# Router columns on two hardware queues, one-hot tiles over eight places, and an earlier x: one edit to a fused attention and expert kernel

## The chip, the cores and the metric

The kernel runs on one core of a Trainium2 chip. The metric is the device time of one execution in microseconds. TensorE (PE) multiplies, VectorE (DVE), ScalarE (ACT) and GpSimd (POOL) work elementwise, and SyncE (SP) mostly issues transfers; ScalarE and GpSimd issue some too.

## The reference

The input x is 2048 rows of 448. One half is 16-head softmax attention (28 columns a head); the other routes every row to two of eight experts. A gate from x mixes them.

```python
g = sigmoid((x * gate_w).sum(-1))
qkv = x @ wqkv; p = softmax(q @ k.T * 28**-0.5); a = (p @ v) @ wo
logits = x @ w_gate                       # 8 columns, one an expert
topk_idx, topk_val = the two largest;  gates = softmax(topk_val)
b = sum over e of w_e * (silu(x @ w1[e]) @ w2[e])    # w1[e] 448x1792, w2[e] 1792x448
out = g * a + (1 - g) * b
```

## The kernel before

Matrix products are computed from high and low halves: ScalarE copies a tile into the type that TensorE multiplies (`_h`, `hi`, `xeh`), VectorE subtracts that from the original (`_l`, `lo`, `xel`), and three products are added up. TensorE's, VectorE's and ScalarE's instructions stand in the order in which the program writes them, in all of the part below. GpSimd's and SyncE's order in this part is made by a scheduler, and it can shift when the program changes.

**Start and projection of v.** Rows of x come in 16 tiles of 128 (`load_x`, on SyncE). Each is transposed on TensorE (`turn_x`) and split. One weight tile `wv_r`, four blocks of rows, holds the v columns of `wqkv` (448), the eight router columns `w_gate`, the gate column `gate_w` and a zero column. `rows4` loads a narrow matrix into the four blocks with three transfers: rows 0 to 383 as 128x3, and rows 384 to 447 twice, since the fourth block holds its 64 rows two times; a last argument picks some of the three. Blocks 0 and 1 of the v columns come over ScalarE's queue, 2 and 3 over SyncE's, router and gate columns over GpSimd's. While this loads, `busy` issues transposes of a constant (7, 3 and 5) between the first two x tiles. ScalarE then splits the four blocks (`wv_h`, L336), VectorE makes their low halves (`wv_low`, L320), and eleven matmuls (L354) make v and the logits of one x tile.

**q and k, with the routing between.** `qk_tile(mt)` makes 128 columns of q and k for all rows in four chunks of 512 rows, eleven matmuls a chunk (L557), into one of four `pq` banks. ScalarE copies the bank (`hi`, L566), and VectorE's difference (`lo`, L569) is put off to the next chunk (`late`, `pop`). In the first 16 chunks (mt 3, 4, 0, 1) there are two places a chunk, behind its second and its fifth matmul, where `pop(1)` and `route(5)` run. `route` takes up to five steps of the generator `routing` and ends early where that yields "pause". `routing` picks two experts for each row, gives each row a slot, and then finds for every slot its row: for two choices and two halves of the tiles it compares a counting row with slot numbers into two one-hot tiles, `ob` (place in a block of 128, L480) and `ot` (block, L484), multiplies `ot` by the tile number on GpSimd (L487) and by the row's place on ScalarE (L489), and after some empty places four batches of eight matmuls (L500) add these up into the index lists.

**The first expert's x.** After these chunks five `gather` transfers fetch the first expert's rows (576 of them), and three more q/k tiles follow (mt 5, 2, 6). In the last one `first_x(c)` runs behind each of its four chunks and turns gathered tiles (`x_tile`, L217): four transposes on TensorE, a copy on ScalarE (L219), and the low halves on VectorE (L159, L160) at the next opportunity.

**Experts and attention.** For each expert there are two halves of seven hidden blocks (L797) and then the second product (L841), with row maxima for the attention (L101, L116) threaded between. w2's tiles come in a ring of nine (L663). Attention follows (L963, L975), then the output product (L921).

Of the kernel before, what the change touches and what calls it, by code (L numbers as in the profile page):

```python
# [24 lines left out]
S, D, H, DH, E, FF = 2048, 448, 16, 28, 8, 1792  # L25
# [19 lines left out]
def bc(ap, shape):  # L45
    return ap.to_broadcast(shape)
# [3 lines left out]
def tile_gated_mha_moe(ctx: ExitStack, tc: tile.TileContext, x, wqkv, wo, wgate, w1, w2, gw, out):  # L50
    nc = tc.nc
# [141 lines left out]
    def rows4(dst, src, eng, parts=slice(0, 3)):  # L193
        for to, rows in ((dst[:, 0:3], src[0:384].rearrange("(b p) n -> p b n", p=128)),
                         (dst[0:64, 3], src[384:448]), (dst[64:128, 3], src[384:448]))[parts]:
            eng.dma_start(to, rows)
# [7 lines left out]
    def first_w():  # L204
        return pe.tile([128, 4, 512], F32, name="wv_r")
# [6 lines left out]
    def x_tile(xg, k, new_pt, xeh, xel):  # L212
        n = CT[k]
        flush_x()
        pt = new_pt()
        for b in range(4):
            nc.tensor.transpose(pt[:, b, :n], xg[:n, b * 128:(b + 1) * 128], ident[:n, :n])  # L217
        h, l = xeh[:, :, k * 128:k * 128 + n], xel[:, :, k * 128:k * 128 + n]
        nc.scalar.activation(h, pt[:, :, :n], AF.Copy)  # L219
        late_x.append(lambda: split_xl(pt, h, l, n))  # L220

    with ExitStack() as pa:
# [8 lines left out]
        def load_x(t):  # L231
            xt = wk.tile([128, 512], F32, name="xt", bufs=NXT)
            nc.sync.dma_start(xt[:, 0:D], x[t * 128:(t + 1) * 128])
            xts.append(xt)

        wv_r = first_w()[:, :, 0:NV]
# [2 lines left out]
        nc.gpsimd.memset(warm, 0.0)  # L239
        load_x(0)  # L240
        load_x(1)
        for b in range(2):
            nc.scalar.dma_start(wv_r[:, b, 0:D], wqkv[b * 128:(b + 1) * 128, 2 * D:3 * D])
        nc.scalar.activation(warm[:, 1:2], warm[:, 0:1], AF.Copy)
        nc.sync.dma_start(wv_r[:, 2, 0:D], wqkv[256:384, 2 * D:3 * D])
        for b in range(2):
# [2 lines left out]
        nc.gpsimd.iota(jp, pattern=[[1, 128]], base=0, channel_multiplier=-1,  # L249
                       allow_small_or_imprecise_dtypes=True)  # L250
        nc.vector.tensor_scalar(ident, jp, 0.0, None, op0=ALU.is_equal)
        rows4(wv_r[:, :, D:D + E], wgate, nc.gpsimd)
        rows4(wv_r[:, :, D + E:D + E + 1], gw.unsqueeze(1), nc.gpsimd, slice(1, 3))
        nc.gpsimd.memset(wv_r[:, :, NV - 1], 0.0)
        for t in range(2, NXT - 1):
            load_x(t)
# [84 lines left out]
        for t in range(NT):  # L341
# [13 lines left out]
            if 4 <= t < 12:  # L355
                b, c = divmod(t - 4, 2)
# [28 lines left out]
        def routing():  # L385
# [90 lines left out]
            for c in range(2):  # L476
                for h in range(2):
                    hs_ = slice(8 * h, 8 * h + 8)
                    ob = wk.tile([128, 8, 128], BF, name="xt", bufs=NXT)
                    nc.vector.tensor_tensor(ob, bc(iob.unsqueeze(1), [128, 8, 128]),  # L480
                                            bc(bb[:, c, hs_].unsqueeze(2), [128, 8, 128]), op=ALU.is_equal)
                    yield
                    ot = sb.tile([128, 8, NTL], BF, name="ot", bufs=2)
                    nc.vector.tensor_tensor(ot, bc(iob[:, 0:NTL].unsqueeze(1), [128, 8, NTL]),  # L484
                                            bc(tb[:, c, hs_].unsqueeze(2), [128, 8, NTL]), op=ALU.is_equal)
                    mv = wk.tile([128, 8, 2, NTL], BF, name="xt", bufs=NXT)
                    nc.gpsimd.tensor_tensor(mv[:, :, 0], ot, bc(iot[:, hs_].unsqueeze(2), [128, 8, NTL]),  # L487
                                            op=ALU.mult)
                    nc.scalar.mul(mv[:, :, 1], ot, iop)  # L489
                    pairs.append((ob, mv))  # L490
                    yield "pause"
            yield "pause"
            yield "pause"
            yield "pause"
            yield "pause"
# [40 lines left out]
            yield "end"  # L536

        rt = routing()

        def route(n):  # L540
# [41 lines left out]
        xe = []  # L582

        def first_x(c):
            for k in ((0, 1), (2,), (3,), (4,))[c]:
                x_tile(xgs[k], k, lambda: ps.tile([128, 4, 128], F32, name="pt"), *xe)

        maxes(1)
# [461 lines left out]
```

## Time and profile before

| What | Value |
|---|---|
| median of 3 runs | 1495.57 us (1494.75 to 1496.4) |
| the profiled execution | 1493.23 us |
| its span, first to last instruction | 1491.4 us |
| TensorE busy | 99% of the span |
| VectorE, ScalarE, GpSimd busy | 54%, 59%, 41% |
| mean granted TensorE clock | 0.996 |

A row of the timeline has the start in us, the length, the engine, the line, the operation, what is written and read, the shape, how often it stands in a row, and in brackets the idle time of the engine before it and what ended that. A q behind an engine's name marks the issue of a transfer. A row of the waits has the engine and line that waited, what it waited for, and total us, times and longest. The chunk numbers in the prediction count the q/k chunks from 0.

### The profile page before, as it was taken

How to read it: one execution, taken by the hardware profiler on the slowest of the kernel's cores; microseconds unless marked ns; L12 is line 12 of the kernel's file. 1: busy time of each engine (PE TensorE's matmuls, PEld its weight loads, DVE VectorE, ACT ScalarE, POOL GpSimd, SP SyncE). 2: the span in 40 equal slices, each digit the busy share in tenths (PEclk: the TensorE clock that was granted, in tenths of full speed). 3: DMA queues.
4: the chain of work that ended last, by engine and by line, in shares of the span. 5: the costliest groups of instructions: out<-in, count | busy, mean ns of one | idle time of the engine just before them, and what ended most of it. 6: DMA issues, size and time to landing. Idle time of an engine off the chain costs nothing. (4 is left out here: it accounts for less than half of the span.)

```text
span 1491.4 us, 28369 instructions
## 1 busy us (share of the span) xinstructions
PE 1473.6 (99%) x11380; PEld 984.5 (66%) x11380; DVE 806.7 (54%) x672; ACT 882.3 (59%) x1539; POOL 613.8 (41%) x667
## 2 busy tenths in 40 slices
PE   8999999999999999999999999899999999999998
PEld 7878788788888887887888888533333333333348
DVE  4644777777768777767777777311122111123245
ACT  5324354344334433543443344399999999999981
POOL 2123575476457546754764565111113111214330
PEclk9999999999999999999999999999999999999999
DMA  9777631343233143313422410300221121143212
GB/s 322 259 250 233 177 96 55 106 123 96 76 120 114 42 124 120 96 54 107 126 84 73 120 60 1 92 21 21 68 66 52 54 66 34 29 112 107 71 37 103
DMA packets 107958, 147.97 MB, mean 99 GB/s; under 512 B 17356, under 2 KB 83308, under 8 KB 107824
## 3 DMA queue, kind: packets, MB, share of 16 engines
q1 hardware_dynamic: 98192, 124.90, 27.0%
q0 software_dynamic: 9344, 20.78, 4.8%
q8 instruction: 90, 1.47, 0.4%
q10 hardware_dynamic: 288, 0.46, 0.1%
q14 instruction: 44, 0.36, 0.1%
HBM read 108.56 MB, written 37.51 MB: 98 GB/s over the span
## 5 line engine op out<-in xcount | busy, mean ns | idle before, releaser
L116 DVE TENSOR_REDUCE mp<-pm 128x6 f32<-128x3072 f32 x171 | 573.1, 3351 | 141.7 <-PE pm L101 141.2
L966 ACT ACTIVATE P<-ps 128x1536 f32<-128x1536 f32 x256 | 370.7, 1448 | 0.0
L975 PE MATMUL po<-P,V 128*32 128x512 f32 x2048 | 273.7, 606 | 0.0
L797 PE MATMUL acc<-xeh,w1l 128*128 128x288 f32 x880 | 258.2, 300 | 0.0
L797 PE MATMUL acc<-xeh,w1h 128*128 128x288 f32 x880 | 257.3, 299 | 0.0
L714 POOL TENSOR_TENSOR w2l<-w2r,w2h 128x448 fp32r<-128x448 f32 x112 | 128.9, 1151 | 235.8 <-ACT w2h L708 204.9
L963 PEld LDWEIGHTS ps<-Q,Kh 29*128 29x128 f32 (+1 forms) x2048 | 79.4, 184 | 216.2 <-ACT P L965 215.7
L799 ACT ACTIVATE hh<-acc 128x288 fp32r<-128x288 f32 x224 | 92.1, 411 | 178.4 <-PE acc L797 178.4
L797 PE MATMUL acc<-xel,w1h 128*128 128x288 f32 x660 | 197.1, 299 | 0.0
L963 PE MATMUL ps<-Q,Kh 29*128 29x512 f32 (+1 forms) x2048 | 192.6, 446 | 1.6 <-ACT P L965 1.5
L930 POOL DMA_DIRECT2D sum_d<-osb x64 | 31.9, 509 | 353.6 <-DVE osb L979 353.6
L797 PEld LDWEIGHTS acc<-xeh,w1l 128*128 128x128 f32 x880 | 166.1, 189 | 14.4 <-issue 14.2
L841 PE MATMUL acc<-w2h,hh 128*128 128x448 f32 x448 | 171.4, 383 | 2.3 <-DMA Kh<-neg_d 2.3
L797 PEld LDWEIGHTS acc<-xeh,w1h 128*128 128x128 f32 x880 | 165.9, 189 | 11.2 <-issue 11.0
L841 PE MATMUL acc<-w2l,hh 128*128 128x448 f32 x448 | 169.3, 378 | 0.0
L841 PE MATMUL acc<-w2h,hl 128*128 128x448 f32 x448 | 165.9, 370 | 0.0
L979 DVE COPY osb<-po 128x512 f32<-128x512 f32 x16 | 11.1, 691 | 283.2 <-PE po L975 283.2
L965 ACT ACTIVATE P<-ps 128x512 f32<-128x512 f32 x256 | 153.0, 598 | 7.0 <-PE ps L963 6.2
L679 POOL TENSOR_TENSOR w1l<-w1r,w1h 128x512 fp32r<-128x512 f32 (+1 forms) x88 | 137.8, 1566 | 19.2 <-ACT w1h L673 6.9
L723 POOL TENSOR_TENSOR hl<-hf,hh 128x512 fp32r<-128x512 f32 x112 | 143.2, 1286 | 0.0
L797 PEld LDWEIGHTS acc<-xel,w1h 128*128 128x128 f32 x660 | 124.7, 189 | 7.9 <-issue 7.7
L101 PE MATMUL pm<-khg,qg 28*128 28x512 f32 x1024 | 124.9, 460 | 1.1 <-DVE mp L116 1.0
(179 smaller groups left out, 1855.3 us busy)
## 6 DMA issues: line engine op xcount, KB each, us to landing
w2r<-in_B_w_dram SPq DMA_DIRECT2D x112, 224.0 KB
w1r<-in_B_w_dram SPq DMA_DIRECT2D x56, 384.0 KB
w1r<-in_B_w_dram SPq DMA_DIRECT2D x112, 64.0 KB
qkh_d<-hi SPq DMA_DIRECT2D x28, 256.0 KB
qkl_d<-lo SPq DMA_DIRECT2D x28, 256.0 KB
ys_d<-yo SPq DMA_DIRECT2D x32, 224.0 KB
ys_d<-zf SPq DMA_DIRECT2D x24, 224.0 KB
v_d<-v_s SPq DMA_DIRECT2D x16, 256.0 KB
```

Of the source, the lines that this page charges most:

```text
L101: nc.tensor.matmul(pm[:, n], qgs[g, qt // 4][rw, (qt % 4) * 128:(qt % 4 + 1) * 128], kh[g, kc][rw], start=True, stop=True)
L116: nc.vector.tensor_reduce(mps[b // 48][:, o:o + len(step)], pm[:, 0:len(step)], axis=AX.X, op=ALU.max)
L679: nc.gpsimd.tensor_tensor(l[:, :, half], r[:, :, half], h[:, :, half].bitcast(F32), op=ALU.subtract)
L714: nc.gpsimd.tensor_tensor(w2l, w2r, w2h.bitcast(F32), op=ALU.subtract)
L723: nc.gpsimd.tensor_tensor(hl, hf32, hh[:, 0:512].bitcast(F32), op=ALU.subtract)
L797: nc.tensor.matmul(pu[:, 0:HC], a, b[:, cs], start=i == 0, stop=i == len(mms) - 1)
L799: nc.scalar.activation(hh[:, cs], pu[:, 0:HC], AF.Silu)
L841: nc.tensor.matmul(py[:n, 0:w], a[:, cs], b, start=i == 0, stop=i == 3 * NH - 1)
L963: nc.tensor.matmul(p3[:, j - 1] if j else p1, k[rw, ks], qs[u][rw, c], start=i == 0, stop=i == 2)
L965: nc.scalar.activation(P[:, 0], p1, AF.Exp, scale=SCALE)
L966: nc.scalar.activation(P[:, 1:4], p3, AF.Exp, scale=SCALE)
L975: nc.tensor.matmul(po[32 * j:32 * j + 32], v[:, kt % 8, 32 * j:32 * j + 32], P[:, j], start=kt == 0, stop=kt == NT - 1)
```

## The change

Three edits. First, of the router's three transfers into `wv_r`, the one for blocks 0 to 2 moves from GpSimd's queue to ScalarE's, between its two weight blocks, and the two for block 3 move to SyncE's, behind block 3 of the weights and ahead of x tile 2. The gate column's last two stay on GpSimd's queue. Second, the one-hot routine pauses after `ob` as well as after `ot`, so that the four pairs are spread over eight places instead of four, and one of the five empty places behind them is gone: the four batches of index matmuls come three places later. Third, `first_x` turns gathered tiles 2 and 3 behind the second chunk and tile 4 behind the third, and none behind the last.

```diff
-        for b in range(2):
-            nc.scalar.dma_start(wv_r[:, b, 0:D], wqkv[b * 128:(b + 1) * 128, 2 * D:3 * D])
+        nc.scalar.dma_start(wv_r[:, 0, 0:D], wqkv[0:128, 2 * D:3 * D])
+        rows4(wv_r[:, :, D:D + E], wgate, nc.scalar, slice(0, 1))
+        nc.scalar.dma_start(wv_r[:, 1, 0:D], wqkv[128:256, 2 * D:3 * D])
...
-        rows4(wv_r[:, :, D:D + E], wgate, nc.gpsimd)
         rows4(wv_r[:, :, D + E:D + E + 1], gw.unsqueeze(1), nc.gpsimd, slice(1, 3))
+        rows4(wv_r[:, :, D:D + E], wgate, nc.sync, slice(1, 3))
...
                     nc.vector.tensor_tensor(ob, bc(iob.unsqueeze(1), [128, 8, 128]),
                                             bc(bb[:, c, hs_].unsqueeze(2), [128, 8, 128]), op=ALU.is_equal)
-                    yield
+                    yield "pause"
...
                     pairs.append((ob, mv))
                     yield "pause"
-            yield "pause"
             yield "pause"
...
         def first_x(c):
-            for k in ((0, 1), (2,), (3,), (4,))[c]:
+            for k in ((0, 1), (2, 3), (4,), ())[c]:
                 x_tile(xgs[k], k, lambda: ps.tile([128, 4, 128], F32, name="pt"), *xe)
```

## The prediction

> **What bounds the kernel now.** I read the page first, then the waits of TensorE, then the timeline of the first 140 us, which is all that the change touches.
>
> ```profile
> PE 1473.6 (99%) x11380; PEld 984.5 (66%) x11380; DVE 806.7 (54%) x672; ACT 882.3 (59%) x1539; POOL 613.8 (41%) x667
> ```
>
> TensorE is busy for 1473.6 of 1491.4 us, and the change neither adds nor removes a matmul. So it can pay only through the 18 us in which TensorE stands, and through the clock. The waits of TensorE say where it stands (total us, times, longest):
>
> ```profile
> PE acc L841 <- DMA Kh<-neg_d: 2.3, 1, 2.3
> PE pq L557 <- DVE lo L569: 2.3, 1, 2.3
> ...
> PE acc L797 <- DVE xeh L160: 1.4, 1, 1.4
> ...
> PE acc L797 <- ACT ht L805: 0.3, 1, 0.3
> PE pq L354 <- DVE xel L320: 0.2, 1, 0.2
> ```
>
> The second row is the one-hot stage, the third the hand-over to the first expert, the last the start: one wait for each part of the change. The first row is the seam before attention, which is not touched. Everything from the first expert on keeps its instructions, so what TensorE gains before it should arrive at the end.
>
> **Part 1, the start.** The timeline, by start and length:
>
> ```profile
> 2.54 1.90 POOL L196 DMA_DIRECT2D wv_r<-in_B_w_gate_dram  x3
> 4.40 1.07 POOL L196 DMA_DIRECT2D wv_r<-in_gate_w_dram  x2
> 5.97 1.06 PE L316 MATMUL pt<-ident,xt 128*128 128x128 f32 x4
> 6.83 1.27 PE L325 MATMUL pq<-ident 128*128 128x128 f32 x5
> 6.93 0.29 DVE L160 TENSOR_TENSOR xh<-pt,xh 64x128 fp32r<-64x128 f32 x1
> 7.64 1.54 ACT L336 ACTIVATE xeh<-wv_r 128x458 fp32r<-128x458 f32 x3 [1.32 <-DMA wv_r<-in_B_w_gate_dram]
> 8.26 1.80 DVE L320 TENSOR_TENSOR xel<-wv_r,xeh 128x458 fp32r<-128x458 f32 x3 [1.03 <-ACT xeh L336]
> 9.02 0.47 PE L354 MATMUL pq<-xel,xh 128*128 128x458 f32 x1
> 10.17 0.37 PE L354 MATMUL pq<-xeh,xh 128*128 128x458 f32 x1
> 10.22 0.59 ACT L336 ACTIVATE xeh<-wv_r 128x458 fp32r<-128x458 f32 x1 [1.05 <-DMA wv_r<-in_gate_w_dram]
> 10.38 0.37 PE L354 MATMUL pq<-xel,xh 128*128 128x458 f32 x1
> 11.85 0.60 PE L316 MATMUL pt<-ident,xt 128*128 128x128 f32 x4
> ```
>
> The router's columns are issued by GpSimd at 2.54 and land at 7.64, where ScalarE has waited 1.32 us for them; the last gate column, issued from 4.40, lands at 10.22, after another 1.05. Without the first wait ScalarE splits blocks 0 to 2 in 6.32 to 7.86. VectorE is free at 6.93+0.29 = 7.22 and starts its three at 0.60 each there instead of at 8.26. But TensorE's filler transposes (L325) run until 6.83+1.27 = 8.10 and do not move. So the first projection matmul moves only to 8.10; the second, at 9.02 now, follows it. TensorE is still at about half speed there: four transposes take 1.06 us at 5.97 and 0.60 at 11.85. I take two matmuls at 0.42 and nine at 0.21 (10.17 to 10.38): 8.10+0.84+1.89 = 10.83, where the next transposes start now at 11.85. Gain 1.0 us.
>
> This needs the fourth block split before the tenth matmul, some 10.4. GpSimd no longer issues the three router transfers, so the two gate transfers move from 4.40 to 2.54; landing 1.9 earlier is 8.3, ScalarE is done at 8.9, VectorE by 9.7. It holds with 0.7 to spare. If only the filler's end counts, the gain is 0.2; that is the lower end, 1.1 the upper.
>
> What pays: ScalarE's queue gets one transfer of 384 rows of 32 bytes between its two weight blocks. No row of this size is on a hardware queue here. The queue itself gives the bound:
>
> ```profile
> q10 hardware_dynamic: 288, 0.46, 6.7%
> ```
>
> That is ScalarE's queue in the first 20 us: 6.7% of 16 engines is 21.4 us for 288 packets, 74 ns for one, nearly all of 1,792 bytes. 384 short rows at no more than 74 ns on 16 engines are 1.8 us; I take 0.5, since they are far shorter, from nothing to 1.8 for the range. The two weight blocks need 21.4/16 = 1.3 us of the engines, twice that beside SyncE's queue, so block 1 is in by about 5 (an estimate) and then by 5.5 to 7; it is wanted at 6.8. SyncE issues two small transfers more ahead of x tiles 2 to 7, some 0.9 us at 0.46 each (4.14 us for nine w2 loads, below); tile 2 is first wanted by the transposes at 11.85. I cost both at nothing, since the cover is the filler on TensorE and the two tiles that are in; with that cover gone up to 0.9 of the 1.0 is given back.
>
> The scheduler also moves two of the first expert's w1 loads from ahead of the v stores to behind them; wanted only from the expert's third hidden block on, they cost nothing, and what they free early I do not count.
>
> The Trainium skill speaks against this edit (DMA: Bandwidth & Descriptors, Specifications): transfers below 512 bytes run under line rate, by a read-modify-write. No run here shows 32-byte rows on these queues.
>
> **Part 2, one-hot tiles over eight places.** Timeline of VectorE, ScalarE and TensorE, then the windows (us, busy of five engines, granted clock, DMA share, GB/s):
>
> ```profile
> 67.92 0.68 DVE L484 TENSOR_TENSOR ot<-iob,tb 128x512 bf16<-128x512 bf16 x1
> 72.47 0.69 DVE L569 TENSOR_TENSOR lo<-pq,hi 128x512 fp32r<-128x512 f32 x1 [1.28 <-ACT hi L566]
> 74.81 1.21 DVE L480 TENSOR_TENSOR xt<-iob,bb 128x1024 bf16<-128x1024 bf16 x1
> 75.94 1.53 DVE L484 TENSOR_TENSOR ot<-iob,tb 128x512 bf16<-128x512 bf16 x1
> 78.75 1.89 DVE L569 TENSOR_TENSOR lo<-pq,hi 128x512 fp32r<-128x512 f32 x3 [1.27 <-ACT hi L566]
> 103.60 0.69 DVE L569 TENSOR_TENSOR lo<-pq,hi 128x512 fp32r<-128x512 f32 x1 [1.80 <-ACT hi L566]
> ```
> ```profile
> 77.51 0.72 ACT L489 ACTIVATE xt<-ot,iop 128x512 bf16<-128x512 bf16 x1 [1.86 <-DVE ot L484]
> 78.14 1.55 ACT L566 ACTIVATE hi<-pq 128x512 fp32r<-128x512 f32 x3
> ```
> ```profile
> 75.13 0.62 PE L500 MATMUL pt<-xt 128*128 128x128 bf16 x8
> 75.56 0.47 PE L557 MATMUL pq<-xh,wqk_l 128*128 128x512 f32 x1
> ...
> 79.49 0.50 PE L557 MATMUL pq<-xh,wqk_h 128*128 128x512 f32 x1 [2.30 <-DVE lo L569]
> ```
> ```profile
> 80.00:82.00 2.00, 2.00 (x13) 1.33 (x13) 1.02 (x3) 0.60 (x1) 0.00 (x0) 0.63 0.98 371
> 82.00:84.00 2.00, 2.00 (x12) 1.81 (x12) 0.30 (x1) 0.00 (x0) 0.00 (x0) 0.51 1.00 381
> ```
>
> A chunk of q/k takes 1.80+0.69 = 2.49 us (steady state). There are four pq banks, so chunk n+4 needs `lo` of chunk n. Now two one-hot pairs stand between two `lo`: on ScalarE the copy `hi` of chunk 5 stands behind the multiply at 77.51, which waits for the `ot` of 75.94. `lo` of chunk 5 is done at 79.4, and chunk 9 stands 2.30 us for it. Behind this the clock is at 0.63 and 0.51: 2 x 0.37 + 2 x 0.49 = 1.7 us lost.
>
> After: `ob`, then `ot`, at places of their own, and one `lo` for each pair. The ring of one chunk is ob 1.21, ot 0.68, multiply 0.72, hi 0.52, lo 0.69: 3.8 us against 2.49, so VectorE still falls behind by 1.3 a chunk, for four chunks. On the old clock `lo` of chunk 4 ends at 67.92+0.68+0.72+0.52+0.69 = 70.5, then 74.3, 78.1 and 82.0 for chunk 7. Chunk 9 would start at 79.49-2.30-0.43 = 76.8 (the batch at 75.13, 0.43 to the next row, comes three places later). Chunk 8 starts at 74.3, chunk 10 at 79.2; chunk 11, with two batches in chunk 10, at 82.6. Chunk 8 has 3.8 us to spare, then 2.5, 1.1 and 0.6. No wait is left, so neither is the slow clock: 2.3+1.7 = 4.0 us. The moved index matmuls put the gathers behind chunk 12 instead of 11, which without the 4 us is no later than now; they are needed only behind chunk 24.
>
> The Trainium skill (TensorE: Matmul & The Clock Gate, Part 1: The HAM clock gate) has the clock fall after an idle window of about 3.4 us, of windows that run freely. By that a 2.3 us wait alone costs no clock and the sum would be 4.1; the trace, with the slow clock right behind the wait, says 5.8.
>
> **Part 3, x a chunk sooner.**
>
> ```profile
> 132.13 0.46 PE L217 MATMUL pt<-ident,xg 64*128 64x64 f32 x4
> 133.58 0.23 DVE L160 TENSOR_TENSOR xeh<-pt,xeh 64x64 fp32r<-64x64 f32 x1
> 133.84 0.69 DVE L569 TENSOR_TENSOR lo<-pq,hi 128x512 fp32r<-128x512 f32 x1
> 133.96 0.37 PE L797 MATMUL acc<-xeh,wv_r 128*128 128x288 f32 x1 [1.36 <-DVE xeh L160]
> 135.88 4.14 SPq L663 DMA_DIRECT2D w2r<-in_B_w_dram  x9
> 138.37 0.58 ACT L708 ACTIVATE w2h<-w2r 128x448 fp32r<-128x448 f32 x1 [1.99 <-DMA w2r<-in_B_w_dram]
> 139.66 0.40 PE L797 MATMUL acc<-xeh,wv_r 128*128 128x288 f32 x1 [0.26 <-ACT ht L805]
> ```
>
> The fifth x tile is turned behind the last q/k chunk, and the expert waits 1.36 us for its split. Turned a chunk sooner, that split hides under 2.49 us of matmuls, and the expert starts 1.36 earlier. Next late is w2: its first load is issued at 135.88, 1.35 after the last `lo`, lands 2.49 later, and ScalarE's split of it stands ahead of the output that frees the accumulator. `lo` no longer stands behind the x split (one half of it is 0.23; I take 0.6 for both halves and their wait). In the built order SyncE's read of the spill count, which stands in the 1.35 us, moves behind w2's loads, and one key load more comes ahead of them. Together w2 comes some 0.8 sooner. TensorE arrives 1.36 sooner: the wait of 0.26 grows to 0.8. Net 0.8 us, from 0.5 (w2 no sooner than its `lo`) to 1.4.
>
> **Sum.** 1.0+4.0+0.8 = 5.8 us. The profiled execution took 1493.23 (span 1491.4), so it would be 1487.4. It lies 2.3 below the median of the timed runs, 1495.57, and I forecast for that: 1489.8.
>
> **The rivals.** One: the wait goes, but the clock had not followed it, or does not in the timed runs because its windows fall otherwise. Then 4.1: 1491.5. For it: how a 2.3 us wait falls on such windows is chance, and the profile is one execution. Against it: the only other wait of 2.3 us, at the seam, is followed by slow clock too.
>
> ```profile
> 954.00:958.00 4.00, 3.55 (x19) 2.07 (x17) 0.62 (x1) 0.42 (x1) 2.34 (x5) 0.57 0.12 38
> ```
>
> Chance 0.18. Two: the ring does not close. The `ot` at 75.94 took 1.53 where another took 0.68; with 0.85 more in each of four rings `lo` of chunk 7 ends at 85.4 and chunk 11 stands 2.8, with the slow clock behind: gain 1.0+0.8-0.5 = 1.3, 1494.3. It decides once a ring is over 0.15 us longer than mine. Against it: the long `ot` is the second of two pairs back to back, with GpSimd's product of the first beside it, and pairs now lie apart. Chance 0.07. Three: only the one-hot part arrives, start and hand-over being made up by transfers: 1491.6, chance 0.05. Four, slower: the short rows clog ScalarE's queue and block 1 comes late. Now it is split by 8.2 (7.64 and one of three); later than that, each us is one of TensorE's. To end 3 us slower against 4.8 from the other parts it must land near 16, eleven us late over 24 rows on each engine: 0.46 us a row against the 74 ns above. Then 1498.6, chance 0.04.
>
> **How the numbers follow.** The forecast keeps 0.66: 1489.8. About 0.2% (3.0 us) is what a measurement can tell, so faster is below 1492.6. Forecast and rivals one and three make 0.89, less 0.05 for a seam whose slow stretches fall differently: 0.84. Same 0.10 (rival two and part of that), slower 0.06. The low end is 1.1+4.0+1.4 with 1.7 for a slow stretch lost at the seam, 8.2: 1487.3, rounded to 1487.0. The high end, 1494.0, reaches nearly to rival two.
>
> **What would show it.** Right: the next transposes near 10.8 instead of 11.85; no row for `lo` among TensorE's waits and a clock of 1.00 from 60 to 100 us; no wait for xeh at the first expert, and one for ht near 0.8. Wrong: a wait for `lo` at chunk 10 or 11, ScalarE waiting for a weight block, or slow clock behind none of these.

## The result and the profile after

The changed kernel takes 1489.51 us (median of seven runs), the kernel before beside it 1494.94: a gain of 5.4 us where 5.8 was forecast. The ratio is 0.9967, 95% interval 0.9956 to 0.9977, which is 3.4 to 6.6 us. One run of the seven was disturbed and is left out of the ratio; the other six lie between 1487.65 and 1492.17, with a median of 1489.35. The profiled execution took 1489.51, its span is 1487.7, 3.7 less than before. The total agrees with the forecast; the parts do not all, and the third did not come.

TensorE's busy time, then its waits (total us, times, longest), in the changed kernel. The wait of L841 is the seam before attention, which was there before:

```profile
PE 1472.2 (99%) x11380; PEld 982.8 (66%) x11380; DVE 805.7 (54%) x672; ACT 883.1 (59%) x1539; POOL 611.7 (41%) x664
...
PE acc L841 <- DMA m_d<-mr: 2.3, 1, 2.3
...
PE acc L797 <- ACT ht L805: 1.4, 1, 1.4
...
PE pq L355 <- DVE xel L321: 0.2, 1, 0.2
```

The rows for `lo` (2.3) and for xeh (1.4) are gone. The wait for ht is 1.4 where it was 0.3 and where I forecast 0.8: a new wait has taken the place of the third edit's.

The start, timeline of the changed kernel (its lines from L243 to L490 are one higher than before):

```profile
1.16 0.45 ACTq L196 DMA_DIRECT2D wv_r<-in_B_w_gate_dram  x1
2.54 1.11 POOL L196 DMA_DIRECT2D wv_r<-in_gate_w_dram  x2
6.78 0.71 PE L326 MATMUL pq<-ident 128*128 128x128 f32 x5
6.98 1.54 ACT L337 ACTIVATE xeh<-wv_r 128x458 fp32r<-128x458 f32 x3 [0.50 <-DMA wv_r<-in_gate_w_dram]
7.62 0.47 PE L355 MATMUL pq<-xeh,xh 128*128 128x458 f32 x1
8.73 0.59 ACT L337 ACTIVATE xeh<-wv_r 128x458 fp32r<-128x458 f32 x1 [0.21 <-DMA wv_r<-in_B_w_gate_dram]
10.49 0.60 PE L317 MATMUL pt<-ident,xt 128*128 128x128 f32 x4
```

The transposes stand at 10.49 instead of 11.85 (forecast 10.83). What ends ScalarE's wait at 6.98 is now the gate column: its first transfer, rows 0 to 383, is issued by GpSimd at 1.28 in both kernels. The filler ends at 6.78+0.71 = 7.49 and not at 8.10: in this execution the clock was full from 6.41, before from 8.85.

The one-hot stage, VectorE and TensorE, and one row of the windows:

```profile
66.55 0.68 DVE L485 TENSOR_TENSOR ot<-iob,tb 128x512 bf16<-128x512 bf16 x1
68.51 0.69 DVE L569 TENSOR_TENSOR lo<-pq,hi 128x512 fp32r<-128x512 f32 x1 [1.28 <-ACT hi L566]
72.22 0.69 DVE L569 TENSOR_TENSOR lo<-pq,hi 128x512 fp32r<-128x512 f32 x1 [1.28 <-ACT hi L566]
75.92 0.69 DVE L569 TENSOR_TENSOR lo<-pq,hi 128x512 fp32r<-128x512 f32 x1 [1.27 <-ACT hi L566]
79.62 1.89 DVE L569 TENSOR_TENSOR lo<-pq,hi 128x512 fp32r<-128x512 f32 x3 [1.28 <-ACT hi L566]
```
```profile
75.10 0.39 PE L557 MATMUL pq<-xh,wqk_h 128*128 128x512 f32 x1
```
```profile
80.00:84.00 4.00, 4.00 (x30) 3.10 (x29) 2.20 (x4) 1.16 (x3) 0.00 (x0) 1.00 0.87 331
```

A ring takes 3.70 us from one `lo` to the next (forecast 3.8), no `ot` takes 1.53 any more, chunk 9 starts at 75.10 without a wait, TensorE is busy for all of 80 to 84 and the clock is 1.00.

The hand-over to the first expert:

```profile
127.07 0.29 PE L797 MATMUL acc<-xeh,wv_r 128*128 128x288 f32 x1
127.95 0.69 DVE L569 TENSOR_TENSOR lo<-pq,hi 128x512 fp32r<-128x512 f32 x1 [1.55 <-ACT hi L566]
129.04 0.87 SPq L85 DMA_DIRECT2D khg<-qkh_d  x2
130.01 4.15 SPq L663 DMA_DIRECT2D w2r<-in_B_w_dram  x9
132.57 0.58 ACT L708 ACTIVATE w2h<-w2r 128x448 fp32r<-128x448 f32 x1 [3.15 <-DMA w2r<-in_B_w_dram]
133.59 0.23 ACT L805 ACTIVATE ht<-acc 128x64 f32<-128x64 f32 x1
133.86 0.40 PE L797 MATMUL acc<-xeh,wv_r 128*128 128x288 f32 x1 [1.40 <-ACT ht L805]
```

The expert starts right behind the last chunk. Then ScalarE stands 3.15 us for w2, with the copies that free the accumulator queued behind that split, and TensorE stands 1.40.

What was won up to here did not all reach the end. Three marks of TensorE (start of the first q/k matmul, from there to the first of chunk 24, from there to the start of the last matmul of L797), in us, for all profiles of this study:

```
kernel                                first q/k  to chunk 24  to last L797
before                                    53.09        67.13        808.58
changed                                   51.72        62.94        808.29
changed, once more                        52.18        62.94        810.25
before + queues alone                     51.59        67.16        809.25
before + one-hot alone                    53.02        62.96        808.49
before + x alone                          53.15        65.58        810.37
before + filler in the wait               53.08        65.58        807.70
before + index matmuls later              52.84        66.11        808.42
changed, x as before                      52.58        62.96        808.36
changed, w2 split later                   51.93        62.93        808.30
changed, gate column moved                52.46        62.93        810.10
changed, both of these                    51.78        62.93        811.12
changed, w2 split later, w1 first         54.48        62.96        806.67
the last, x as before                     51.56        62.96        807.79
```

In the changed kernel's profile that is 1.37+4.19+0.29 = 5.85 us up to the last of L797, and 3.7 at the end. Part of the 2.1 between is the clock at the seam. First a row of the kernel before, then the changed kernel in windows cut where the clock changes:

```profile
961.00:965.00 4.00, 4.00 (x32) 1.17 (x28) 0.00 (x0) 2.48 (x4) 1.89 (x2) 0.57 1.00 204
```
```profile
945.08:948.49 3.41, 1.23 (x6) 1.16 (x7) 0.00 (x0) 1.28 (x1) 0.00 (x0) 1.00 0.15 38
948.49:951.90 3.41, 3.06 (x17) 1.63 (x15) 0.62 (x1) 0.32 (x1) 2.24 (x5) 0.50 0.12 38
951.90:955.32 3.42, 2.41 (x20) 1.51 (x24) 0.00 (x0) 3.03 (x4) 3.12 (x7) 0.50 0.89 222
955.32:958.73 3.41, 3.41 (x28) 1.00 (x24) 0.00 (x0) 2.47 (x3) 1.58 (x2) 0.50 1.00 211
```

Three windows of 3.41 us are at half clock, where the profile before has two (954.35 to 957.76 and 961.17 to 964.59). A whole window of matmuls at half clock costs 1.7 us, but TensorE stands for 1.4 us of these three. Compared at the same matmul, the changed kernel loses 0.7 us at the seam, 0.9 in attention, where its profile has two waits for `P` (at 1346.42 and 1373.47) that the one before has not, and the last 0.6 in the output product, whose matmuls follow each other a little more slowly. Why the last two losses came is open. How the seam falls matters in every comparison: two profiles of this study have no slow window there (x alone, and the filler below), and they come out of it 2.8 and 2.9 us sooner than the one before.

### The profile page after: what moved, and what is told of

Read it like the earlier page. It is cut to its first block, busy times and chain, and to the rows that moved or that the text cites. A ratio compares the mean times of both kernels' runs of the same rounds, so it can differ in the third digit from the quotient of the medians.

```text
span 1487.7 us, 28372 instructions
## 1 busy us (share of the span) xinstructions
PE 1472.2 (99%) x11380; PEld 982.8 (66%) x11380; DVE 805.7 (54%) x672; ACT 883.1 (59%) x1539; POOL 611.7 (41%) x664
## 3 DMA queue, kind: packets, MB, share of 16 engines
q8 instruction: 90, 1.47, 0.4%
## 5 line engine op out<-in xcount | busy, mean ns | idle before, releaser
L797 PE MATMUL acc<-xeh,w1l 128*128 128x288 f32 x880 | 258.0, 300 | 0.0
L797 PE MATMUL acc<-xeh,w1h 128*128 128x288 f32 x880 | 257.2, 299 | 0.0
L797 PE MATMUL acc<-xel,w1h 128*128 128x288 f32 x660 | 197.0, 298 | 0.0
L797 PEld LDWEIGHTS acc<-xeh,w1l 128*128 128x128 f32 x880 | 166.0, 189 | 14.4 <-issue 14.2
L841 PE MATMUL acc<-w2h,hh 128*128 128x448 f32 x448 | 171.3, 382 | 2.3 <-DMA m_d<-mr 2.3
L797 PEld LDWEIGHTS acc<-xeh,w1h 128*128 128x128 f32 x880 | 165.8, 188 | 11.2 <-issue 11.0
L841 PE MATMUL acc<-w2l,hh 128*128 128x448 f32 x448 | 169.0, 377 | 0.0
L841 PE MATMUL acc<-w2h,hl 128*128 128x448 f32 x448 | 165.7, 370 | 0.0
L797 PEld LDWEIGHTS acc<-xel,w1h 128*128 128x128 f32 x660 | 124.6, 189 | 7.9 <-issue 7.7
```

The costliest lines, as they stand in the source:

```text
L797: nc.tensor.matmul(pu[:, 0:HC], a, b[:, cs], start=i == 0, stop=i == len(mms) - 1)
L841: nc.tensor.matmul(py[:n, 0:w], a[:, cs], b, start=i == 0, stop=i == 3 * NH - 1)
```

## The experiments

Each ratio is to the kernel before that ran beside it. It is not the quotient of the two medians given, and can differ from that by about 0.001.

**The one-hot edit alone** (kernel before).

```diff
-                    yield
+                    yield "pause"
...
-            yield "pause"
```

> The kernel before with the one-hot edit alone. Theory (the wait for lo at chunk 9 goes and the slow clock behind it too): no row for lo among TensorE's waits, granted clock 1.00 from 60 to 100 us, chunk 24 starts about 4.0 us sooner than before's 120.22, time 4.0 us below before (ratio 0.9973). Rival (the slow clock at 80 us is not the wait's doing): the wait goes, a slow stretch of 3.4 us stays somewhere between 70 and 90 us, 2.3 us below before (0.9985). The start stays at 11.85 us for the second set of transposes, the expert still waits about 1.4 us for xeh.

Measured: 1489.2 against 1492.57, ratio 0.9966 (0.9952 to 0.9979). No wait for `lo`, 62.96 us from the first q/k matmul to chunk 24 instead of 67.13, which is 4.17. This part carries most of the gain. Whether the clock belongs to it, the next runs tell.

**The queues alone** (kernel before with the first block of the diff).

> The kernel before with the edit of the queues alone. Theory (the first projection matmul follows the gate column and the filler, not the router's columns): ScalarE's first split of a weight block starts near 7.0 us instead of 7.64, the second set of transposes starts at 10.5 to 10.8 us instead of 11.85, chunk 9 still waits about 2.3 us for lo, and 1.0 to 1.4 us below before (ratio 0.9991 to 0.9993). Rival (the start is set by where the first clock window falls, not by the transfers): the transposes' place differs from 11.85 by as much as the clock's change to full speed differs, and the time is that of before within 0.5 us.

Measured: 1491.71 against 1492.57, ratio 0.9990 (0.9981 to 0.9999). The first split starts at 6.88, the transposes at 10.38, and the first q/k matmul 1.5 sooner. The rival is out: in four profiles without this edit the clock was full by 6.74 and the transposes still stood at 11.60 to 11.91. The landing scatters, though: in five profiles with the edit the first split started at 6.83 to 7.15, in two at 7.86 and 8.19, as late as before.

**x alone** (kernel before).

```diff
-            for k in ((0, 1), (2,), (3,), (4,))[c]:
+            for k in ((0, 1), (2, 3), (4,), ())[c]:
```

> The kernel before with the first expert's x turned a chunk sooner, alone. Theory (w2's landing behind ScalarE's in-order split takes the gain back): the first expert matmul starts 1.3 us sooner relative to the last q/k chunk, but its fourth group of matmuls waits about 1.4 us for ht instead of 0.26, so net 0.2 to 0.3 us. Rival (as I forecast it): w2 lands 0.8 us sooner, the wait for ht is 0.8, net 0.8 us; at most 1.4 if no later wait grows.

Measured: 1493.44 against 1492.57, ratio 1.0004 (0.9995 to 1.0014): no gain. The wait for ht was 2.08, and the clock was at half behind it. The same profile shows a second thing. Here are windows of 3.41 us, cut where the clock can change, of the kernel before, of the queues alone and of x alone; all three wait 2.3 us for `lo`:

```profile
77.12:80.53 3.41, 1.11 (x12) 0.77 (x11) 2.14 (x4) 2.18 (x4) 1.04 (x1) 1.00 0.26 99
80.53:83.95 3.42, 3.42 (x17) 2.61 (x15) 0.79 (x2) 0.60 (x1) 0.00 (x0) 0.50 1.01 382
```
```profile
75.28:78.70 3.42, 1.11 (x6) 0.42 (x5) 2.15 (x4) 2.18 (x4) 1.20 (x2) 1.00 0.22 81
78.70:82.11 3.41, 3.41 (x21) 2.73 (x19) 1.14 (x2) 0.60 (x1) 0.00 (x0) 0.50 0.99 375
```
```profile
74.48:77.90 3.42, 2.78 (x18) 1.84 (x16) 3.08 (x3) 1.03 (x2) 2.11 (x2) 1.00 0.44 124
77.90:81.31 3.41, 1.73 (x13) 1.20 (x13) 1.89 (x3) 2.19 (x5) 0.83 (x1) 1.00 0.46 176
81.31:84.72 3.41, 3.41 (x28) 2.75 (x28) 1.31 (x2) 0.88 (x2) 0.00 (x0) 1.00 1.01 381
...
135.92:139.34 3.42, 1.34 (x10) 1.11 (x9) 2.90 (x1) 2.02 (x7) 1.34 (x2) 1.00 0.91 273
139.34:142.75 3.41, 3.41 (x16) 3.25 (x14) 0.00 (x0) 2.09 (x7) 2.52 (x3) 0.50 0.88 314
```

The second column is TensorE's busy time, the third from the right the clock. In the first two kernels the wait lies in one window (1.11 busy, 2.30 idle), and the next window is at half clock. In the third the window's edge cuts it into 0.64 and 1.68, and the clock stays full. The wait for ht, 2.08 idle in one window, is followed by half clock. So the 1.7 us are the wait's doing, but only where the wait falls into one window.

**A filler in the wait** (kernel before).

```diff
+                if (mt, c) == (0, 1):
+                    fill = ps.tile([128, 4, 128], F32, name="pt")
+                    for b in range(16):
+                        nc.tensor.transpose(fill[:, b % 4], ident, ident)
```

> The kernel before with 16 transposes of the identity (0.15 us each at full clock, 2.4 us) put into TensorE's order ahead of chunk 9, into a buffer nobody reads: they fill the wait for lo and leave its length. Theory (the slow clock at 80.5 to 83.9 us follows from the idle TensorE): chunk 9 starts at about 79.5 as before, the granted clock stays at 1.00 from 60 to 100 us, and chunk 12 starts 1.7 us sooner than before's 90.30; 1.7 us below before (ratio 0.9989). Rival (the slow stretch has another cause, for example where the clock's windows fall): the slow stretch stays, time as before within 0.3 us.

```profile
77.02 1.91 PE L554 MATMUL pt<-ident 128*128 128x128 f32 x16
79.51 0.50 PE L561 MATMUL pq<-xh,wqk_h 128*128 128x512 f32 x1 [0.58 <-DVE lo L573]
```

Measured: 1490.55 against 1492.57, ratio 0.9982 (0.9973 to 0.9991). The 16 transposes took 1.91, chunk 9 starts at 79.51 as before, the clock stays at 1.00, chunk 12 starts at 88.74 instead of 90.30. The profile alone does not prove the point: an edge of its windows, at 78.39, cuts the wait, and in x alone that was enough to keep the clock without a filler. The runs speak for the filler: the mean granted clock is 0.9984 over its 11 and 0.9972 over the 27 of the kernel before beside them, and the difference is about one slow window (1.7/1490 = 0.0011). Work that computes nothing made the kernel faster, and the clock accounts for it.

**The index matmuls three places later, the pairs as before** (kernel before with three more empty places).

> The kernel before with the index matmuls three places later, as the changed kernel has them, and the one-hot pairs still over four places. Theory (the pairs' places close the ring, the index matmuls have no part in it): chunk 9 still waits for lo, 2.3 us and the 0.4 of the batch that now comes behind it, 2.7 in all; chunk 9 starts at 79.5, nothing gained (ratio 0.9995 to 1.0005). Rival (it was the index matmuls' move that gave TensorE's time back): the wait shrinks under 1 us and 1.5 us or more are gained.

```profile
PE pq L560 <- DVE lo L572: 2.9, 1, 2.9
```

Measured: 1495.18 against 1495.23, ratio 1.0004 (0.9994 to 1.0014). The wait is still there, so the later index matmuls do not end it by themselves; the pairs' places do, alone or with them. In this profile too an edge cuts the wait (1.39 and 1.47 us of standing in two windows), and the clock stays full.

**The changed kernel once more.**

> The changed kernel once more, on the same chip as the three below, for the scatter of its clock and of w2's landing. Theory (the clock is granted in windows of 3.41 us whose place differs from run to run, and is halved for the window behind one in which TensorE stood for about 2 us or more): no slow window from 60 to 100 us wherever the windows fall, since there is no wait; at the seam near 945 to 960 us one to three slow windows or none, by whether the 2.2 us in which TensorE stands there falls into one window. Rival (slow windows come at random): one between 60 and 130 us as likely as anywhere. Time about 5 us below before (ratio 0.9955 to 0.9977).

Measured: 1488.32 against 1493.91, ratio 0.9961 (0.9948 to 0.9975). The wait for ht was 1.91 in this profile, and it cost clock too:

```profile
132.08:135.49 3.41, 1.50 (x12) 1.27 (x11) 3.12 (x1) 1.95 (x7) 1.26 (x2) 1.00 0.97 317
135.49:138.91 3.42, 3.42 (x17) 3.41 (x15) 0.00 (x0) 2.16 (x7) 2.43 (x3) 0.50 0.82 279
```

My expectation had none between 60 and 100, which held, and left out this place.

**The first w2 split behind the outputs of the first hidden block** (changed kernel).

```diff
-                            split_w2_high(i2)
+                            if i2:
+                                split_w2_high(i2)
...
+                            if not i2:
+                                split_w2_high(i2)
```

> The changed kernel, with ScalarE's split of the first expert's first w2 block moved behind the outputs of its first hidden block (nothing left out). Theory (the hand-over's gain is lost because the copies that free the accumulator stand on ScalarE behind a split that waits for w2): the wait for ht (1.40 us in the changed kernel's profile, 2.1 and 1.0 in two others) goes, the block behind it starts 5.9 us after the first expert matmul instead of 6.79, and 1.0 to 1.4 us below the changed kernel (about 6.5 below before, ratio 0.9955 to 0.996). Rival (the next thing is as late, w1's second block or the second w2 block): the wait moves to the next block of matmuls and the time is the changed kernel's within 0.3 us.

```profile
132.83 0.58 ACT L708 ACTIVATE w2h<-w2r 128x448 fp32r<-128x448 f32 x1 [1.17 <-DMA w2r<-in_B_w_dram]
133.49 1.15 POOL L714 TENSOR_TENSOR w2l<-w2r,w2h 128x448 fp32r<-128x448 f32 x1 [22.84 <-ACT w2h L708]
134.59 1.27 POOL L679 TENSOR_TENSOR w1l<-w1r,w1h 128x512 fp32r<-128x512 f32 x1
135.92 0.40 PE L797 MATMUL acc<-xeh,w1l 128*128 128x288 f32 x1 [1.32 <-POOL w1l L679]
```

Measured: 1487.89 against 1493.91, ratio 0.9962 (0.9949 to 0.9976), the changed kernel's. The wait for ht is gone, and 1.32 us of waiting for w1l stand a block later: the rival was right. On GpSimd the same thing happens as on ScalarE; w1's piece stands behind w2's piece, which waits for w2.

**GpSimd's piece of w1 first as well** (the kernel above, with `split_w2_low` of the first block behind `split_w1_low`).

```diff
-                    split_w2_low(i2)
+                    if i2:
+                        split_w2_low(i2)
                     if ahead:
                         split_w1_low(ahead, HALVES[ft % 2])
+                    if not i2:
+                        split_w2_low(i2)
```

> The changed kernel with ScalarE's split of the first w2 block behind the outputs of the first hidden block, and GpSimd's part of that split behind its part of w1's second block (same work, other order). Theory (both engines work in order, and each had a piece that TensorE needs standing behind a piece that waits for w2): no wait for ht and none over 0.4 us for w1l in the first expert, its first 44 matmul groups end 1.3 us sooner than with the first move alone, no slow clock between 130 and 140 us; 1.4 us below the changed kernel and more where that had a slow window, about 6.5 to 7 below before (ratio 0.9953 to 0.9957). Rival (w1's second half or the second w2 block is as late): a third wait of 1 us or more shows up in the first 10 us of the expert and the time is the changed kernel's within 0.5 us.

```profile
132.00:136.00 4.00, 4.00 (x31) 3.47 (x31) 1.84 (x1) 2.15 (x7) 1.30 (x1) 1.00 0.85 268
136.00:140.00 4.00, 4.00 (x31) 3.35 (x30) 2.87 (x2) 2.96 (x10) 3.99 (x4) 1.00 0.95 305
```

Measured: 1487.24 against 1495.23, ratio 0.9950 (0.9936 to 0.9963), the lowest ratio of the study, though the interval overlaps those of the kernels near it. TensorE stands nowhere in the hand-over, and chunk 24 to the last of L797 takes 806.67 against 808.29 and 810.25 in the two profiles of the changed kernel. This profile had a bad start (first split 8.19, half clock behind it), so its span of 1487.6 does not show it.

**That kernel with x turned as before.**

> The kernel with both reorderings of the split of w2 (the last one but two above), with x turned where the kernel before turns it. Theory (the earlier turn is worth its 1.36 us once nothing behind it waits for w2, and nothing before that): the wait of 1.36 us for xeh is back, no wait for ht or over 0.4 us for w1l; from the first matmul of chunk 24 to the last of L797 808.0 us, against 806.7 with the earlier turn and 808.5 in the kernels with neither; 1.3 us above the kernel with the reorderings (ratio to before 0.9955 to 0.996). Rival (the reorderings alone bring all of it, the turn nothing even then): 806.7 us and the time of the kernel with the reorderings within 0.3 us.

```profile
PE acc L797 <- DVE xeh L160: 1.4, 1, 1.4
```

Measured: 1487.14 against 1492.52, ratio 0.9963 (0.9949 to 0.9976), 807.79 us for the last part. The earlier turn is worth 1.1 us here (807.79-806.67) in the traces; the times, with intervals of 0.13%, can't tell the two apart.

**The changed kernel with x turned as before.**

> The changed kernel with the first expert's x turned where it was before: the start's and the one-hot edits stay. Theory (the earlier turn brings nothing, it only moves the wait): a wait of 1.36 us for xeh, a wait for ht of 0.3 to 1.0, the block behind ht starts 19.2 to 20.2 us after chunk 24, as with the earlier turn; no slow window at 130 to 140 us, since the two waits fall apart; time the changed kernel's within 0.5 us or below it, about 5.5 below before (ratio 0.996). Rival (the turn is worth the 0.8 us that I forecast): 0.8 us above the changed kernel.

Measured: 1488.66 against 1495.23, ratio 0.9964 (0.9951 to 0.9978), as with the turn. xeh waits 1.36, ht 0.25, and 808.36 us for the last part.

**The gate column on ScalarE's queue** (changed kernel) and **this with the later w2 split**.

```diff
-        rows4(wv_r[:, :, D + E:D + E + 1], gw.unsqueeze(1), nc.gpsimd, slice(0, 1))
...
         rows4(wv_r[:, :, D:D + E], wgate, nc.scalar, slice(0, 1))
+        rows4(wv_r[:, :, D + E:D + E + 1], gw.unsqueeze(1), nc.scalar, slice(0, 1))
```

> The changed kernel, with the first transfer of the gate column (384 rows of 4 bytes) on ScalarE's queue behind the router's columns instead of GpSimd's. Theory (at the start the gate column, which lands at 6.98 us, is now the last to arrive): ScalarE's first split of a weight block starts at 6.5 us, right behind its split of x, the second set of transposes near 10.0 us instead of 10.49 and 10.38; 0.4 us below the changed kernel, which the times can hardly tell. Rival (the short rows hold up the second weight block on the same queue): ScalarE's split of that block starts later than 7.47 us and the transposes come no sooner than 10.4.

> The changed kernel with both further edits: the first w2 split behind the outputs of the first hidden block, and the gate column's first transfer on ScalarE's queue. If both theories hold, 1.4 to 1.8 us below the changed kernel, 6.5 to 7.3 below before (ratio 0.995 to 0.9957). If neither does, the changed kernel's time within 0.3 us.

```profile
6.77 0.59 ACT L337 ACTIVATE xeh<-wv_r 128x458 fp32r<-128x458 f32 x1 [0.91 <-DMA wv_r<-in_gate_w_dram]
7.67 1.54 ACT L337 ACTIVATE xeh<-wv_r 128x458 fp32r<-128x458 f32 x3 [0.32 <-DMA wv_r<-in_A_wqkv_dram]
```

Measured: 1488.75 against 1493.91, ratio 0.9963 (0.9950 to 0.9977), and 1490.61, ratio 0.9976 (0.9967 to 0.9986). The rival was right: the column lands little sooner, and the second weight block behind it on the queue is wanted at 7.36 and comes at 7.67. With both edits the wait for w1l (1.3) and one for the copy of the accumulator (1.2) lie close, and half clock followed.

## Why the prediction came out, point by point

**The start.** Forecast 1.0, with TensorE's filler as the new bound. The filler was the wrong bound: its end moves with the clock (7.05 to 8.28 over the profiles), and the first weight block is complete later than I took it. Of the seven profiles with the edit, ScalarE's wait for that block is ended by the gate column in five, whose first transfer I had not costed. In four of these and in the one below, the second set of transposes follows the first split by 3.49 to 3.58 us, whether the filler ends at 7.05 or at 8.10; in the fifth it is 3.81, and there the clock was not full before 9.20. Without the edit the first q/k matmul starts at 52.84 to 53.15 in five profiles, with it at 51.56 to 52.58 in six and at 54.48 in one: the size was about right, the reason was not, and the scatter of the landing was left out. It can hit the moved transfers too. In the profile of the changed kernel with x as before, the router's columns on their new queue were what ScalarE waited for, as late as without the edit; in the profile with 54.48 the trace names a tile of x (8.19), and what was late there is open.

```profile
7.86 2.21 ACT L337 ACTIVATE xeh<-wv_r 128x458 fp32r<-128x458 f32 x4 [1.60 <-DMA wv_r<-in_B_w_gate_dram]
```

The price of the short rows in the DMA engines' time was about right. ScalarE's queue in the first 20 us:

```profile
q10 hardware_dynamic: 688, 0.47, 10.2%
```

That is 400 packets and 3.5% of 16 engines more, 11.2 us, 28 ns a packet; the six other profiles with the edit have 8.2 to 9.6%, which is 12 to 23 ns. It makes 0.3 to 0.7 us of the engines, and I took 0.5. By the Trainium skill (DMA: Bandwidth & Descriptors, Specifications) transfers under 512 bytes run below line rate; they do, at 32 bytes in 12 to 28 ns against 1,792 in 74, and with so few packets it took little of the engines.

**The one-hot stage.** The ring and the end of the wait were right, and so was the spare time of `lo` for chunks 8 to 11 (3.4, 2.2, 1.0 and 0.9 us; forecast 3.8, 2.5, 1.1 and 0.6): from the first q/k matmul to chunk 24 it is 62.93 to 62.96 us in every kernel with the edit. The term that was mis-sized is the clock's 1.7 us. The wait can cost it, as I took it, but of the four profiles that have the wait in full only two have it (before and the queues alone, and not x alone and the later index matmuls). What is sure is 65.58-62.94 = 2.6 us; with the slow window it is 4.2. Rival one named this, with its right reason: how the wait falls on the windows is chance.

**The hand-over.** Here the step failed. The 1.36 us went as forecast (the expert starts 1.33 sooner against chunk 24), but "w2 comes some 0.8 sooner" did not: ScalarE's split of w2 started 0.25 us sooner. `lo` was 0.33 us sooner against chunk 24, where I took 0.6; from its end to w2's issue it took 1.37 us where it had taken 1.35, since two key loads stand there in place of the read of the spill count (how often the overflow loop runs); and the landing took 2.56 instead of 2.49. So the wait came to 1.40, and to 1.9, 2.1 and 1.9 in the three other profiles with the turn and the split in its old place. In those three it was long enough for half clock. From chunk 24 to the last of L797 the changed kernel takes 808.29 and 810.25 with the earlier turn and 808.36 without it; x alone takes 810.37 where before takes 808.58. So in the traces the third edit brought at most 0.1 us and cost up to 1.9, instead of bringing 0.8. The times alone show no difference (0.9964 without it, 0.9961 and 0.9967 with it).

**The sum.** That 5.4 came where 5.8 was forecast is luck in part. In the pair of profiles the parts are 1.4, 4.2 and 0.3, where I had 1.0, 4.0 and 0.8, and the second holds the clock's 1.7, which is a matter of chance. Of their 5.85 only 3.7 arrived, although I took it that what is gained before the experts arrives at the end. In the timed runs the start's 1.15 (between the medians of those starts) and the wait's 2.6 make 3.8 of the 5.4. That lies within the interval of 3.4 to 6.6; how the rest divides between the clock and scatter, no run here shows. Nor does the mean granted clock of the runs settle it, of which one slow window is 0.0011. Against the kernel before beside it, the changed kernel has 0.9968 to 0.9965, the one-hot edit alone 0.9978 to 0.9972, and the changed kernel with x as before 0.9980 to 0.9965. That would fit a slow window lost behind `lo` and another got behind ht. But x alone has 0.9973 to 0.9972, and the changed kernel with the gate column moved, which keeps the turn, 0.9982 to 0.9965; these do not show the one behind ht.

## What to carry to other kernels

A wait taken away in front of an in-order engine is only worth what the next late thing leaves: look for work that waits for a transfer and has the copies that free an accumulator, or another operand, queued behind it, and put those first. Two waits of 1.4 and 0.3 us can be cheaper than one of 1.9 (808.36 against 810.25 us for the last part), because, by the cases in the next section, what counts is how long TensorE stands within one window. Cost the clock's share of a wait as a chance, and read it from several profiles.

## What was not expected of the hardware

The clock is granted in windows of 3.41 us, whose edges lay at a different place against the program's start in each execution (the remainder of the edge's time by 3.41 ran from 0.13 to 3.40 in 14 profiles). Where TensorE stood for 1.87 us or more of one window, the next was at half clock: 15 cases of 15. At 1.56 to 1.83 two of six were (1.56 and 1.64, and not 1.63, 1.68, 1.75 and 1.83), so there is no clean limit in that range, and what else decides is open. This leaves out attention (from 948.6 to 955.9 us on, by the profile), whose matmuls use 28 or 29 rows: there windows with 0.35 and 1.0 us of standing were followed by half clock as well (the rows of the seam above), so something else counts there. The Trainium skill (TensorE: Matmul & The Clock Gate, Part 1: The HAM clock gate) has the free-running window and its length right; that it takes an idle window does not hold here, half of one was enough.

How soon w2 comes depends on an order that the program does not fix. In the six kernels with neither the earlier turn nor a reordering, ScalarE's first split of w2 starts 17.4 to 18.9 us behind chunk 24. Most of that is SyncE's order as the scheduler built it: the first w2 load is issued at 14.76 us in one, 15.65 or 15.66 in four and 16.35 in one, and the split starts 2.5 to 2.7 later in each. The landing scatters too: in the two profiles of the changed kernel the load is issued at 15.35 and 15.34, and the split starts at 17.91 and 18.42. With waits of 1.4 to 2 us at stake, one profile does not tell an edit's worth, and an edit's effect on the built order has to be read before its effect on the wait.
